# TensorE products whose results nobody reads, placed ahead of waits in the tail of a decode block

## The chip, the cores and the metric

The kernel runs on one core of one Trainium2 chip. The metric is the device time of one execution in microseconds, as the median of several runs. All data are 32-bit floats.

## What is computed

One token passes through an attention block with a cached context and then through a bilinear feed-forward block. The context has 65536 positions, 8 key/value heads and 32 query heads of 128 elements; the model width is 512 and the feed-forward width 1792.

```python
x = A_x
h = x + _A_ref(_layernorm(x, axis=-1), A_k_cache, A_v_cache, A_wq, A_wo)
h2 = h + _B_ref(_layernorm(h, axis=-1), B_w_gate, B_w_up, B_w_down)
...
    scores = jnp.einsum("bhqd,bhkd->bhqk", q, k) * (Dh ** -0.5)
    p = _softmax(scores, axis=-1)
    o = jnp.einsum("bhqk,bhkd->bhqd", p, v)
...
    g = jnp.einsum("bsd,df->bsf", x, w_gate)
    u = jnp.einsum("bsd,df->bsf", x, w_up)
    h = g * u
    return jnp.einsum("bsf,fd->bsd", h, w_down)
```

## The kernel before

**The stream.** Everything that the kernel reads from device memory goes through SyncE's queue in one fixed order into two large buffers, `kv[0]` and `kv[1]`, of 8 MB each: for each of the 8 heads four pieces of keys and four of values, in turn. A piece is issued when TensorE has finished with the buffer. The last piece of values comes in four parts (`V_CUTS`). Behind it come the feed-forward weights: the gate weights in one transfer, the up weights `wu` in three (`U_CUTS`, rows 0 to 2, 2 to 3, 3 to 4 of four), both into `kv[0]` (L153, L156), and the down weights `wd` in five (`D_CUTS`, chunks 0 to 6, 6 to 10, 10 to 12, 12, 13 of fourteen) into `kv[1]` (L160). Each part has its own semaphore (`s_wu`, `s_wd`).

**The heads.** A loop of eight passes runs on TensorE alone. In a pass the keys are multiplied (L346), VectorE and ScalarE make the softmax, its weights are transposed on TensorE into the banks `ptp` (L361), the values are multiplied (L374), and the head's output is turned and projected (L381, L387).

**The tail.** After the last head one chain remains. VectorE adds the rows up (L280); TensorE turns the row into a column and takes off the mean (L396, L398); the gate weights are multiplied (L409 with `psc[1]`); one product makes the variance (L415), ScalarE and VectorE the scale. The up weights are multiplied (L409 with `psc[0]`), four products for each of four rows `k`, with a wait for a weight piece ahead of rows 0, 2 and 3. VectorE multiplies the two rows in two halves (L303); that product is the gated row. TensorE turns it into columns (L421, L425, L428), VectorE copies these into `f_pad` (L307, L309), and the down weights are multiplied: fourteen chunks `c` of four products each, four column blocks of the array side by side (L439), with a wait ahead of each piece. VectorE copies the result (L311), and SyncE writes it out (L313).

A 32-bit product appears in the trace as two matmul records, each with a weight load. So the 56 down products are 112 records, eight for a chunk, and four up products are eight records. Transposes have one record.

Of the kernel before, what the change touches and what calls it, by code (L numbers as in the profile page):

```python
# [24 lines left out]
P = 128  # L25
# [14 lines left out]
V_CUTS = (0, 16, 24, 28, 32)  # L40
U_CUTS = (0, 2, 3, 4)
D_CUTS = (0, 6, 10, 12, 13, 14)


M_Q, M_K, M_MX, M_MB, M_T, M_L, M_V, M_PO, M_AT, M_HEAD = 1, 2, 6, 7, 8, 12, 13, 17, 18, 18
# [14 lines left out]
def body(nc, xc, xr, kT, v, wq0, wqo, wo7, wg, wu, wd, out):  # L60
    pe_e, dve_e, act_e, pool_e, sp = nc.tensor, nc.vector, nc.scalar, nc.gpsimd, nc.sync

    def tile(name, *shape):
        return nc.alloc_sbuf_tensor(name, list(shape), F32).ap()

    def bank(name):
        return nc.alloc_psum_tensor(name, [P, 512], F32).ap()
# [5 lines left out]
    ident, mean_m, ones, neg_mean = (tile(n, P, P) for n in ("ident", "mean_m", "ones", "neg_mean"))  # L73
# [8 lines left out]
    zeros = tile("zeros", P, 512)  # L82
# [15 lines left out]
    ptp = [bank(f"ptp{i}") for i in range(2)]  # L98
# [5 lines left out]
    def sem(name):  # L104
        sems.append(nc.alloc_semaphore(name))
        return sems[-1]
# [7 lines left out]
    s_wu = [sem(f"s_wu{i}") for i in range(len(U_CUTS) - 1)]  # L114
    s_wd = [sem(f"s_wd{i}") for i in range(len(D_CUTS) - 1)]
    s_x, s_xr, s_out = sem("s_x"), sem("s_xr"), sem("s_out")
# [3 lines left out]
    def pe_at(h, m):  # L120
        return M_HEAD * h + m
# [35 lines left out]
    sp.wait_ge(pe.sem, pe_at(LAST, M_V + 3))  # L157
    for p, (lo, hi) in enumerate(zip(D_CUTS, D_CUTS[1:])):
        cs = slice(lo * D, hi * D)
# [159 lines left out]

    mm = pe_e.matmul  # L320

    def take(s, n=1):
        pe_e.wait_ge(s, n).then_inc(s, -n)  # L323

# [4 lines left out]
    mm(sm[1][:, 0:1], mean_m, ln_s2, start=True, stop=True).then_inc(pre, 1)  # L329
    pe_e.wait_ge(dve.sem, c_const)  # L330
    take(s_wq, 16)

    def head():
        for r in range(REP):
            for k in range(KT):
                i = mm(sm[0][:, r:r + 1], wq_sb[:, k, r * P:(r + 1) * P], xn[:, k:k + 1],  # L336
                       start=(k == 0), stop=(k == KT - 1))
        i.then_inc(pe.sem, 1)
        take(tok)
        for s in range(NT):  # L340
            take(s_kv[s % 2], 16)
            if s >= 2:
                take(tok)
            for rs in range(8):
                for j in range(4):
                    i = mm(psc[s % 2][32 * j:32 * j + 32, :],  # L346
                           q_pad[:, 28 - 4 * rs:60 - 4 * rs],
                           kv[s % 2][:, (4 * rs + j) * 512:(4 * rs + j + 1) * 512],
                           start=(rs == 0), stop=(rs == 7))
            i.then_inc(pe.sem, 1)  # L350
# [50 lines left out]
    def project(acc, w, sems):  # L401
        for k in range(KT):
            if len(sems) == 1 and k == 0:
                pe_e.wait_ge(sems[0], 16)
            elif len(sems) > 1 and k in U_CUTS:
                pe_e.wait_ge(sems[U_CUTS.index(k)], 16)
            for j in range(4):
                o = k * F + j * FJ
                i = mm(acc[32 * j:32 * j + 32, :FJ], hn_pad[:, k, :], w[:, o:o + FJ],  # L409
                       start=(k == 0), stop=(k == KT - 1))  # L410
        i.then_inc(pe.sem, 1)

    project(psc[1], wg_t, [s_wg])
    pe_e.wait_ge(dve.sem, c_s3)
    mm(sm[0][:, 0:1], mean_m, ln_s3, start=True, stop=True).then_inc(pe.sem, 1)  # L415
    for j in range(4):
        mm(pva[32 * j:32 * j + 32, 0:P], sel_pad, arow[:, j * P:(j + 1) * P], start=True, stop=False)
    project(psc[0], wu_t, s_wu)
    pe_e.wait_ge(dve.sem, c_f[0])
    for b in range(2):  # L420
        i = mm(sm[0][:, 4 * b:4 * b + 4], f_sb[:, b * P:(b + 1) * P], sel_q,  # L421
               start=(b == 0), stop=(b == 1))
# [4 lines left out]
    for i in range(2):  # L427
        i2 = mm(sm[1][64 * i:64 * i + 64, 4:6], f_sb[:, 3 * P:FJ], sel_q[:, 2 * i:2 * i + 2],  # L428
                start=False, stop=True)
    i2.then_inc(pe.sem, 1)  # L430
    pe_e.wait_ge(dve.sem, c_fp0)
    for c in range(NC):
        if c == 8:
            pe_e.wait_ge(dve.sem, c_fp1)
        if c in D_CUTS:
            pe_e.wait_ge(s_wd[D_CUTS.index(c)], 16)
        for j in range(4):
            o = c * D + j * P
            i = mm(pva[32 * j:32 * j + 32, 0:P], f_pad[:, c, :], wd_t[:, o:o + P],  # L439
                   start=False, stop=(c == NC - 1))  # L440
# [43 lines left out]
```

## Time and profile before

| | us |
|---|---|
| median of 3 runs (lowest to highest) | 1312.81 (1312.80 to 1312.94) |
| the profiled execution's own time | 1313.45 |
| its span, from the first to the last instruction | 1312.1 |
| TensorE matmul busy in the span | 717.8 |
| mean granted TensorE clock, as a share of full speed | 0.732 |

The profile shows one execution on the core. Its own time is 1.35 us longer than the span, which starts with the first instruction and ends with the last. [...] An end of a matmul record is modelled, and lies some tenths of a microsecond after the next product could start.

### The profile page before, as it was taken

What the parts mean: (1) busy time and instruction counts of PE and PEld (TensorE: products, weight loads), DVE (VectorE), ACT (ScalarE), POOL (GpSimd) and SP (SyncE); (2) the same over time, 40 slices, a digit from 0 to 9 for tenths busy, and PEclk for the clock granted to TensorE, in tenths of its full rate; (3) what the DMA queues carried; (4) which work ended last, traced back from release to release, by engine and by line L of the source; (5) the groups of instructions that cost most, each with busy time, mean ns of one, the idle gap of its engine ahead of it and who ended that gap; (6) DMA issues with size and microseconds to landing.
All of it is one profiled execution on the core that took longest, in us unless ns stands there. A gap on an engine that the chain in (4) does not pass through costs nothing. (4 is left out here: it accounts for less than half of the span.)

```text
span 1312.1 us, 10526 instructions
## 1 busy us (share of the span) xinstructions
PE 717.8 (55%) x4922; PEld 249.1 (19%) x4922; DVE 73.3 (6%) x180; ACT 47.2 (4%) x102; POOL 2.5 (0%) x13
## 2 busy tenths in 40 slices
PE   4355374553755446563574736735465454645657
PEld 3011031210312112120131201312121111211213
DVE  0000000100001000010000100001000010000101
ACT  0010000100001000010000100001000010000100
POOL 0000000000000000000000000000000000000000
PEclk9777676786767867767767767668677677777677
DMA  9999999999999999999999999999999999999998
GB/s 416 436 424 446 422 440 424 440 424 440 440 428 442 426 438 426 438 428 438 440 428 440 428 438 426 438 428 438 438 432 436 430 422 441 438 428 438 438 414 356
DMA packets 12405, 564.80 MB, mean 430 GB/s; under 512 B 1510, under 2 KB 1514, under 8 KB 2155
## 3 DMA queue, kind: packets, MB, share of 16 engines
q1 hardware_dynamic: 12248, 564.67, 99.6%
q8 instruction: 6, 0.10, 0.0%
q10 hardware_dynamic: 146, 0.00, 0.0%
q14 instruction: 5, 0.03, 0.0%
HBM read 564.66 MB, written 0.00 MB: 430 GB/s over the span
## 5 line engine op out<-in xcount | busy, mean ns | idle before, releaser
L346 PE MATMUL psc<-kv,q_pad 128*32 128x512 f32 x2048 | 296.8, 744 | 257.0 <-PEq L323 257.0
L374 PE MATMUL pva<-kv,pt 128*16 128x512 f32 x2048 | 283.1, 714 | 272.9 <-PEq L323 272.7
L346 PEld LDWEIGHTS psc<-kv,q_pad 128*32 128x32 f32 x2048 | 81.6, 133 | 465.7 <-issue 465.7
L374 PEld LDWEIGHTS pva<-kv,pt 128*16 128x16 f32 x2048 | 67.5, 111 | 492.0 <-issue 492.0
L224 ACT COPY sc<-psc 128x512 f32<-128x512 f32 x32 | 18.8, 586 | 1146.2 <-PE psc L346 1146.2
L230 DVE TENSOR_REDUCE mx<-sc 128x1 f32<-128x512 f32 x32 | 21.9, 686 | 541.2 <-ACT sc L224 541.2
L336 PE MATMUL sm<-xn,wqo_sb 128*128 128x1 f32 x256 | 48.8, 325 | 2.2 <-issue 2.2
L336 PEld LDWEIGHTS sm<-xn,wqo_sb 128*128 128x128 f32 x256 | 48.1, 293 | 9.6 <-issue 9.6
L264 DVE COPY orow<-pva 128x512 f32<-128x512 f32 x8 | 5.5, 692 | 566.6 <-PE pva L374 566.6
L361 PE MATMUL ptp<-ident,sc 128*128 128x128 f32 x128 | 29.2, 395 | 10.2 <-PEq L323 9.7
L361 PEld LDWEIGHTS ptp<-ident,sc 128*128 128x128 f32 x128 | 21.3, 201 | 15.5 <-issue 14.8
L249 ACT ACTIVATE sc<-sc,nbias 128x512 f32<-128x512 f32 x32 | 22.7, 711 | 20.2 <-DVE nbias L244 20.2
L254 DVE COPY pt<-ptp 128x512 f32<-128x512 f32 x32 | 22.1, 692 | 21.5 <-PE ptp L361 21.5
L366 PE MATMUL pva<-zeros 128*32 128x512 f32 x64 | 13.8, 948 | 0.0
L387 PE MATMUL attn<-wqo_sb,o_pad 128*32 128x512 f32 x64 | 10.9, 756 | 3.3 <-PEq L323 3.3
L381 PE MATMUL sm<-sel_b,orow 128*128 128x4 f32 x64 | 8.2, 252 | 7.2 <-PEq L323 7.2
L381 PEld LDWEIGHTS sm<-sel_b,orow 128*128 128x128 f32 x64 | 7.7, 191 | 14.4 <-issue 14.4
L352 PE MATMUL sm<-ident,m 128*1 128x128 f32 x8 | 2.2, 269 | 13.7 <-PEq L323 13.7
L364 PE MATMUL sm<-l,ones 128*128 128x4 f32 x16 | 4.1, 324 | 9.6 <-PEq L323 9.6
L409 PE MATMUL psc<-kv,hn_pad 128*32 128x448 f32 x64 | 8.9, 702 | 0.6 <-DMA kv<-in_wu 0.3
L439 PE MATMUL pva<-kv,f_pad 128*32 128x128 f32 x112 | 6.1, 416 | 1.1 <-DMA kv<-in_wd 1.1
L354 PE MATMUL sm<-ones,mexp 1*128 1x1 f32 x16 | 3.3, 276 | 5.7 <-PEq L323 5.7
(83 smaller groups left out, 67.7 us busy)
## 6 DMA issues: line engine op xcount, KB each, us to landing
wqo_sb<-in_wqo SPq DMA_DIRECT2D x7, 2048.0 KB, 14.0
kv<-in_v SPq DMA_DIRECT2D x1, 4096.0 KB, 22.5
kv<-in_wg SPq DMA_DIRECT2D x1, 3584.0 KB, 18.0
kv<-in_v SPq DMA_DIRECT2D x1, 2048.0 KB, 27.0
kv<-in_v SPq DMA_DIRECT2D x2, 1024.0 KB, 30.0
kv<-in_wu SPq DMA_DIRECT2D x1, 1792.0 KB, 22.4
kv<-in_wu SPq DMA_DIRECT2D x2, 896.0 KB, 24.9
kv<-in_wd SPq DMA_DIRECT2D x1, 1536.0 KB, 20.1
```

The costliest lines, as they stand in the source:

```text
L224: copies.append(act.tick(act_e.copy(sc[s], psc[s % 2])))
L230: i = dve_e.tensor_reduce(out=mx[:, s:s + 1], in_=sc[s], axis=AX.X, op=ALU.max)
L249: act_e.activation(sc[s], sc[s], AF.Exp, bias=nbias[:, 0:1], scale=SCALE, accum_out=sums[:, s:s + 1]).then_inc(atok, 1)
L254: dve_e.tensor_copy(pt[s].rearrange("p g b h -> p b g h"), ptp[s % 2].rearrange("p (b g h) -> p b g h", b=4, h=REP)).then_inc(tok, 1)
L336: i = mm(sm[0][:, r:r + 1], wq_sb[:, k, r * P:(r + 1) * P], xn[:, k:k + 1], start=(k == 0), stop=(k == KT - 1))
L346: i = mm(psc[s % 2][32 * j:32 * j + 32, :], q_pad[:, 28 - 4 * rs:60 - 4 * rs], kv[s % 2][:, (4 * rs + j) * 512:(4 * rs + j + 1) * 512], st ...
L361: i = pe_e.transpose(ptp[s % 2][:, b * P:(b + 1) * P], sc[s][:, b * P:(b + 1) * P], ident)
L366: mm(pva[32 * j:32 * j + 32, :], zeros[:, 0:32], zeros, start=True, stop=False)
L374: i = mm(pva[32 * j:32 * j + 16, :], pt[n][:, 8 * j + rs, :, :].rearrange("p b h -> p (b h)"), vt[:, w * 512:(w + 1) * 512], start=False, ...
L381: i = mm(sm[0][:, 0:REP], orow[:, b * P:(b + 1) * P], sel_b[:, 4 * b:4 * b + 4], start=(b == 0), stop=(b == 3))
L387: i = mm(attn[32 * r:32 * r + 32, :], o_pad[:, r, :], wo_sb[:, r, :], start=True, stop=True)
L409: i = mm(acc[32 * j:32 * j + 32, :FJ], hn_pad[:, k, :], w[:, o:o + FJ], start=(k == 0), stop=(k == KT - 1))
```

## The change

A function `fill(n)` issues `n` products of the identity matrix (stationary, 128x128) with 128 columns of zeros, into the transpose bank `ptp[0]`, which nothing reads in the tail. Fills are put ahead of waits on TensorE: 2 before the wait for up row 2, 3 before that for up row 3, 3 before the wait for the gated row, 4 before that for its first columns in `f_pad`, and 1, 0, 1 and 4 before those for the second to the fifth piece of the down weights. No wait is added, and no other engine's program is changed.

```diff
+U_FILL = (0, 2, 3)
+F_FILL = 3
+D_FILL = (4, 1, 0, 1, 4)
...
+    def fill(n):
+
+
+        for _ in range(n):
+            mm(ptp[0][:, 0:P], ident, zeros[:, 0:P], start=True, stop=True)
...
             elif len(sems) > 1 and k in U_CUTS:
+                fill(U_FILL[U_CUTS.index(k)])
                 pe_e.wait_ge(sems[U_CUTS.index(k)], 16)
...
     project(psc[0], wu_t, s_wu)
+    fill(F_FILL)
     pe_e.wait_ge(dve.sem, c_f[0])
...
     i2.then_inc(pe.sem, 1)
+    fill(D_FILL[0])
     pe_e.wait_ge(dve.sem, c_fp0)
     for c in range(NC):
         if c == 8:
             pe_e.wait_ge(dve.sem, c_fp1)
         if c in D_CUTS:
+            if c:
+                fill(D_FILL[D_CUTS.index(c)])
             pe_e.wait_ge(s_wd[D_CUTS.index(c)], 16)
```

On TensorE, from the up product to the last down product, the program before reads as follows (`psc` is the bank of the up product, `sm` that of the turned gated row, `pva` the result, `kv` the weights; a row with "waits" holds its semaphores).

```order
L409 MATMUL psc<-kv,hn_pad 32x448 [waits s_wu1]
L409 MATMUL psc<-kv,hn_pad 32x448 x3
L409 MATMUL psc<-kv,hn_pad 32x448 [waits s_wu2]
L409 MATMUL psc<-kv,hn_pad 32x448 x3
L421 MATMUL sm<-sel_q,f_sb 128x4 [waits dve]
...
L428 MATMUL sm<-sel_q,f_sb 64x2 x2
L439 MATMUL pva<-kv,f_pad 32x128 [waits s_wd0,dve]
L439 MATMUL pva<-kv,f_pad 32x128 x23
L439 MATMUL pva<-kv,f_pad 32x128 [waits s_wd1]
```

The same engine and place in the changed program, where each line below the new function has a number that is 10 to 15 higher (L330 is the product in `fill`):

```order
L330 MATMUL ptp<-zeros,ident 128x128 x2
L420 MATMUL psc<-kv,hn_pad 32x448 [waits s_wu1]
L420 MATMUL psc<-kv,hn_pad 32x448 x3
L330 MATMUL ptp<-zeros,ident 128x128 x3
L420 MATMUL psc<-kv,hn_pad 32x448 [waits s_wu2]
L420 MATMUL psc<-kv,hn_pad 32x448 x3
L330 MATMUL ptp<-zeros,ident 128x128 x3
L433 MATMUL sm<-sel_q,f_sb 128x4 [waits dve]
...
L440 MATMUL sm<-sel_q,f_sb 64x2 x2
L330 MATMUL ptp<-zeros,ident 128x128 x4
L454 MATMUL pva<-kv,f_pad 32x128 [waits s_wd0,dve]
L454 MATMUL pva<-kv,f_pad 32x128 x23
```

The fills stand ahead of the waiting products, so they start without waiting for what these wait for, and the products behind them start after them.

The end of TensorE's program, with the last three pieces of the down weights, in the changed kernel:

```order
L454 MATMUL pva<-kv,f_pad 32x128 [waits s_wd2]
L454 MATMUL pva<-kv,f_pad 32x128 x7
L330 MATMUL ptp<-zeros,ident 128x128
L454 MATMUL pva<-kv,f_pad 32x128 [waits s_wd3]
L454 MATMUL pva<-kv,f_pad 32x128 x3
L330 MATMUL ptp<-zeros,ident 128x128 x4
L454 MATMUL pva<-kv,f_pad 32x128 [waits s_wd4]
L454 MATMUL pva<-kv,f_pad 32x128 x3
```

Before, the same rows stand there as L439 without the two rows of L330; nothing has changed places. In all 18 fills are added, 36 matmul records.

## Rows read from the trace of the kernel before

**Rows 1.** The page: span, granted clock and transfers in 40 slices, memory traffic.
```profile
span 1312.1 us, 10526 instructions
...
PEclk9777676786767867767767767668677677777677
DMA  9999999999999999999999999999999999999998
...
HBM read 564.66 MB, written 0.00 MB: 430 GB/s over the span
```

**Rows 2.** The chain that ended last: start us, us, what.
```profile
1283.72 20.06 DMA kv<-in_wd
...
1303.91 6.12 PE pva L439 x112
...
1310.06 0.29 DVE y L311
```

**Rows 3.** Timeline of the tail: start, us, engine, line, output and inputs, records.
```profile
1284.56 1.03 PE L381 MATMUL sm<-sel_b,orow 128*128 128x4 f32 x8 [0.89 <-PEq L323]
...
1297.38 2.44 PE L409 MATMUL psc<-kv,hn_pad 128*32 128x448 f32 x24
...
1300.14 0.96 PE L409 MATMUL psc<-kv,hn_pad 128*32 128x448 f32 x8 [0.32 <-DMA kv<-in_wu]
1301.25 0.81 DVE L303 SCALAR_TENSOR_TENSOR f_sb<-psc,ln_r,g_sb 128x256 f32<-128x256 f32 x2 [3.55 <-PE psc L409]
...
1301.79 0.61 PE L421 MATMUL sm<-sel_q,f_sb 128*128 128x4 f32 x4 [0.69 <-DVE f_sb L303]
...
1302.55 0.28 PE L428 MATMUL sm<-sel_q,f_sb 128*64 128x2 f32 x4
1302.88 0.17 DVE L309 COPY f_pad<-sm 128x6 f32<-128x6 f32 x1 [0.28 <-PE sm L428]
...
1303.91 6.08 PE L439 MATMUL pva<-kv,f_pad 128*32 128x128 f32 x112 [1.08 <-DMA kv<-in_wd]
```

**Rows 4.** The down weights' transfers: issue times, and us from issue to landing.
```profile
L160 SPq DMA_DIRECT2D kv<-in_wd x5: 328/432/433, 1283.7 to 1285.5; - x5
...
DMA to landing us min/median/max: 20.1/23.0/23.3
```

**Rows 5.** Timeline of SyncE's queue: starts of the second and the fourth issue.
```profile
1284.09 0.91 SPq L160 DMA_DIRECT2D kv<-in_wd  x2
...
1285.04 0.91 SPq L160 DMA_DIRECT2D kv<-in_wd  x2
```

**Rows 6.** Transfers by issue: second, third and fourth down piece, us to landing last.
```profile
kv<-in_wd SPq DMA_DIRECT2D x1, 1024.0 KB, 22.2
...
kv<-in_wd SPq DMA_DIRECT2D x1, 512.0 KB, 23.0
...
kv<-in_wd SPq DMA_DIRECT2D x1, 256.0 KB, 23.1
```

**Rows 7.** The up weights' transfers, as in group 4.
```profile
L156 SPq DMA_DIRECT2D kv<-in_wu x3: 432/432/432, 1273.4 to 1274.3; - x3
...
DMA to landing us min/median/max: 22.4/24.1/25.8
```

**Rows 8.** Stretches: length, busy of PE, PEld, DVE, ACT, POOL, then granted clock, DMA.
```profile
1282.50:1285.80 3.30, 2.08 (x16) 1.13 (x16) 0.80 (x2) 0.00 (x0) 0.00 (x0) 1.00 1.01 434
...
1291.40:1296.00 4.60, 4.60 (x28) 1.28 (x32) 0.28 (x2) 0.00 (x0) 0.00 (x0) 0.50 0.97 404
1296.40:1299.80 3.40, 3.40 (x42) 1.19 (x34) 0.16 (x1) 0.90 (x2) 0.00 (x0) 1.00 1.04 435
1299.80:1302.80 3.00, 1.99 (x22) 1.10 (x18) 0.98 (x3) 0.00 (x0) 0.00 (x0) 1.00 0.97 410
1303.00:1309.60 6.60, 5.68 (x108) 5.64 (x112) 0.05 (x1) 0.00 (x0) 0.00 (x0) 0.50 0.63 247
```

**Rows 9.** Transposes (L361) of the last head in a stretch: PE, PEld, granted clock, DMA.
```profile
1218.40:1220.40 2.00, 1.94 (x8) 1.41 (x8) 0.50 1.06 459
```

## The prediction

> **What bounds the kernel now.** I read the page first: the transfers are busy in nine tenths or more of every slice but the last, 430 GB/s over the span [rows 1]. The kernel is bound by one stream of 565 MB, and nothing in the diff touches it. So the change can only work behind the stream's end, and I looked there with the chain of waits. It says that after the first down piece has landed (1283.72 + 20.06 = 1303.78) one thing alone sets the end: 6.12 us of down products, then the copy and the write [rows 2]. About 2 us pass from the copy's start at 1310.06 to the span's end at 1312.1.
>
> Is that stage held by its own work or by the later pieces? The issues start at 1284.09 and 1285.04 for the second and fourth piece [rows 5], so the third starts half way, at 1284.56, and the fifth at 1285.5 [rows 4]. With their times to landing [rows 4, 6] the pieces land at 1306.29, 1307.56, 1308.14 and 1308.8. The products go without a gap from 1303.91 for 6.08 us, fourteen chunks at 0.434 us [rows 3]; they reach chunks 6, 10, 12 and 13 at 1306.51, 1308.25, 1309.12 and 1309.55, always after the piece. So TensorE's own pace sets the end, but the last piece is not far ahead: by 0.75 us.
>
> The stretches say why the pace is what it is. [...] At full clock a chunk should take half, 0.217 us; rows at both levels say so for the up product: the gate products before 1296 run at half the pace of the up products behind them (28 records in 4.6 us against 42 in 3.4, some of these small) [rows 8].
>
> **The price of a fill.** The trace has no such product. It is two passes of 128 columns with a 128-column weight load each. A down chunk is also two passes of 128 columns (four column blocks side by side): 0.434 us cold, 0.217 us warm. Does the wider load add to it? Eight transposes, with loads and columns of this size, took 1.94 us at half clock, 0.243 us each with the run-out of the last one in it [rows 9]. So the loads lie beside the products. At full clock, products with such loads and almost no columns took 1.03 us for eight records [rows 3], 0.129 a pass, 0.26 a fill. I take 0.22 warm and 0.44 cold, since the transposes are nearest in shape. The bounds: 0.26 by the load row; if load and columns did not overlap, 0.129 + 0.109 a pass, 0.47 a fill; and nothing, where waits cover every fill.
>
> **Up stage.** From two rows of up products (three rows `k` and a run-out are 2.44 us, one row and a run-out 0.96 [rows 3]) a row takes 0.74 us. Before, row 2 starts at 1297.38 + 1.48 = 1298.86 and its piece has been there since about 1298: the second issue, half way between 1273.4 and 1274.3, and 24.1 us [rows 7]. So the first two fills fall in no wait and cost 0.44 us in full. Row 2 then runs from 1299.30 to 1300.04, three fills to 1300.70. Piece 3 landed at 1274.3 + 25.8 = 1300.1 [rows 7]; row 3 starts at 1300.70 instead of 1300.14. **The gated row is 0.56 us later.** Row 3 ends at 1301.44, the next three fills at 1302.10; VectorE's first half is done for TensorE at 1301.79 + 0.56 = 1302.35, so these three are hidden with 0.25 us to spare.
>
> **Down stage.** The last turning products end at 1302.55 + 0.28 + 0.56 = 1303.39. Four fills take 0.88 us, to 1304.27. By then the first piece is there (1303.78), and so are both copies into `f_pad` (1302.88 + 0.17 + 0.56 = 1303.61). The first chunk starts 0.36 us later than before. If the clock has stayed up: six chunks (1.30) to 1305.57, a fill to 1305.79, wait for the piece: 1306.29 and the 0.13 us that lay between landing and product before, 1306.42. Four chunks to 1307.29, wait to 1307.56 + 0.13 = 1307.69, two chunks to 1308.12, a fill to 1308.34 (the piece is there at 1308.27), a chunk to 1308.56. Now four fills, 0.88 us, to 1309.44, though the last piece has been usable since 1308.93: half a microsecond given away. The last chunk ends at 1309.66. Before it was 1303.91 + 6.08 = 1309.99. **Gain 0.33 us.**
>
> With a fill at 0.26 the same count ends at 1309.86 (gain 0.13), with fills at nothing at 1308.93 + 0.22 = 1309.15 (gain 0.84). At 0.47 the three hidden fills become late too (row 3 ends at 1302.69, fills at 1304.10 against 1303.60), the down stage starts at 1307.02 and ends at 1312.88, a loss of 2.9 us; the transposes' row speaks against that price.
>
> The profiled execution took 1313.45 us, span 1312.1 and 1.35 around it; by the sum that is 1313.1. It was 0.64 above the median of the runs shown, so the median goes from 1312.81 to 1312.5.
>
> **Rivals.** 0.2% of this kernel, about what a measurement can tell from no change, is 2.6 us.
>
> (a) *Nothing to win back.* In the median run the clock may not have fallen where it did in the profiled one. The profiled time is 0.64 above the median; a down stage at full clock, waiting only for pieces, would end at 1309.15, 0.84 earlier, which is of this size. Then the fills only cost: 1309.66 against 1309.15, 0.5 us slower (0.7 with a fill at 0.26), 1313.3 to 1313.5. For it: the falls near 1285.8 and after 1302.8 followed stretches of nearly the same busy share, so a small shift of the moment could change the case. Against it: three runs within 0.14 us.
> [...]
>
> (b) *The fills don't hold the clock, and only delay* (the other side). If products of zeros don't keep it up, it falls at 1302.8 as before. From 1303.39 four cold fills (1.76) put the first chunk at 1305.15; every chunk takes 0.434, every fill 0.44, and no piece is waited for: 1305.15 + 14 x 0.434 + 6 x 0.44 = 1313.87. That is 3.9 us slower, 1316.7, or 0.3%. It decides if the clock falls before about 1304.5 and stays down. Against: the fills add eight products, 1.76 us at full clock, between 1298.9 and 1302.1, where TensorE had 1.99 of 3 us, much of it in loads and run-outs; stretches as full as that had the clock up [rows 8].
> [...]
>
> (c) *The last piece sets the end.* With the clock up the stage could be bound by landings; then 1309.15, 0.84 us faster, 1312.0. The four fills before the last piece speak against it, unless a fill takes under 0.1 us.
>
> **How the numbers follow.** Forecast, clock held and fills mostly paid (1311.9 to 1312.8 for it alone): 0.50. (a) 0.33. (c) 0.06. (b) 0.05. The rest, 0.06, is for a stream that runs differently in another program, as likely to be shorter as longer. No case but (b), its price bound and half of that rest reaches 0.2% either way: faster 0.03, same 0.92, slower 0.05. The range takes in (c) with the spread of the runs below it, 1311.7, and (a) with the same above it, 1313.8.
>
> **What would show it.** In the trace after: granted clock 1.0 from the up product to the end of the down products; row 3 of the up product some 0.56 us later beside its transfer; the turning products 0.56 us later; chunks at 0.22 us with two short waits for pieces; the last four fills ending after the last piece has landed; a copy of the result 0.1 to 0.8 us earlier. The prediction is wrong if the clock falls in the down stage in spite of the fills, if a fill takes 0.4 us or more at full clock, or if the time moves by more than 2.6 us, which the tail can't give.

## The result and the profile after

The changed kernel took **1314.47 us** (median of 22 runs, 1313.82 to 1316.11) against 1312.78 us (22 runs, 1312.53 to 1313.12): ratio 1.0014, 95% interval 1.0008 to 1.0020. It is 1.7 us slower. That is less than 0.2% of the kernel, but clear of the noise, on the other side of the forecast, and 0.7 us above the range. The profiled execution took 1314.29 us, span 1313.0 us.

The chain that ended last in the changed kernel, from the up product on (start, us, what; `ptp L330` are fills, `psc L420` the up product, `pva L454` the down product):

```profile
1297.69 1.50 PE psc L420 x16
1299.19 0.64 PE ptp L330 x4
1299.83 0.89 PE psc L420 x8
1300.72 0.86 PE ptp L330 x6
1301.59 0.89 PE psc L420 x8
1302.48 0.86 PE ptp L330 x6
1303.34 0.43 PE sm L433 x4
1303.78 0.22 PE sm L437 x2
1304.00 0.21 PE sm L440 x4
1304.21 1.09 PE ptp L330 x8
1305.30 1.45 PE pva L454 x48
1306.75 0.42 PE ptp L330 x2
1307.17 1.45 PE pva L454 x48
1308.61 0.42 PE ptp L330 x2
1309.03 0.36 PE pva L454 x8
1309.39 1.09 PE ptp L330 x8
1310.48 0.40 PE pva L454 x8
```

Where the chain of before began with a transfer [rows 2], this one has no transfer and no wait: TensorE works from the up product to the end, two fifths of the time on fills. The forecast had the gated row 0.56 us later than before; it is 1.39 us later (L433 starts at 1303.18 in the timeline, L421 stood at 1301.79 [rows 3]). The first down chunk is 1.3 us later instead of 0.36. Four starts in the timeline of the changed kernel, which the rest goes by (first up product, first turning product, first and last down chunk; in the chain above the same work starts some hundredths to tenths later):

```profile
1297.50 1.69 PE L420 MATMUL psc<-kv,hn_pad 128*32 128x448 f32 x16
...
1303.18 0.60 PE L433 MATMUL sm<-sel_q,f_sb 128*128 128x4 f32 x4
...
1305.23 1.52 PE L454 MATMUL pva<-kv,f_pad 128*32 128x128 f32 x48
...
1310.41 0.43 PE L454 MATMUL pva<-kv,f_pad 128*32 128x128 f32 x8
```

A count of records tells what a fill costs. One fill has two records; groups of 1, 2, 3 and 4 took 0.42, 0.64, 0.86 and 1.09 us. That is 0.22 us a fill, as forecast, **plus 0.2 us for the group**. The up rows ahead of a group took 0.89 us instead of 0.74: the fills start when the product before them has all but run out (at 1299.12 in the timeline, where the up product's modelled end is 1297.50 + 1.69 = 1299.19). The load unit shows the same place (timeline of weight loads; the bracket is its idle time before):

```profile
1299.12 0.52 PEld L330 LDWEIGHTS ptp<-zeros,ident 128*128 128x128 f32 x4 [0.73 <-issue]
1299.76 0.16 PEld L420 LDWEIGHTS psc<-kv,hn_pad 128*32 128x32 f32 x8
...
1306.68 0.30 PEld L330 LDWEIGHTS ptp<-zeros,ident 128*128 128x128 f32 x2 [0.20 <-issue]
```

The first load of a fill starts at the moment at which the fill itself is shown to start, and the load unit idles until then, 0.73 and 0.20 us. So in this trace the load was not fetched while the products before it ran, and the next up row's load in turn started behind the loads of the fills, at 1299.76 with its product.

The clock and the transfers of the changed kernel, in two views (stretches, with the granted clock third from the end; issues and landings of the down weights):

```profile
1301.60:1305.20 3.60, 3.60 (x32) 2.73 (x32) 1.15 (x4) 0.00 (x0) 0.00 (x0) 1.00 0.98 406
1305.30:1310.80 5.50, 5.50 (x124) 4.30 (x124) 0.00 (x0) 0.00 (x0) 0.00 (x0) 1.00 0.36 137
```

```profile
L164 SPq DMA_DIRECT2D kv<-in_wd x5: 328/432/433, 1284.0 to 1285.8; - x5
...
DMA to landing us min/median/max: 19.7/22.6/23.0
```

The clock is at 1.0 to the end, as forecast, where rows 8 had 0.5. The last piece lands at 1285.8 + 23.0 = 1308.8 us, the same as before. Its product starts 1.6 us later.

### The profile page after: what moved, and what is told of

Same layout as the page of the kernel before. It is cut to its first block, busy times and chain, and to the rows that moved or that the text cites. A ratio compares the mean times of both kernels' runs of the same rounds, so it can differ in the third digit from the quotient of the medians.

```text
span 1313.0 us, 10598 instructions
## 1 busy us (share of the span) xinstructions
PE 719.7 (55%) x4958; PEld 251.3 (19%) x4958; DVE 73.3 (6%) x180; ACT 47.2 (4%) x102; POOL 2.5 (0%) x13
## 5 line engine op out<-in xcount | busy, mean ns | idle before, releaser
L391 PE MATMUL sm<-sel_b,orow 128*128 128x4 f32 x64 | 8.5, 256 | 7.2 <-PEq L333 7.2
L391 PEld LDWEIGHTS sm<-sel_b,orow 128*128 128x128 f32 x64 | 8.0, 196 | 14.4 <-issue 14.4
L420 PE MATMUL psc<-kv,hn_pad 128*32 128x448 f32 x64 | 8.7, 671 | 0.3 <-DVE hn_pad L290 0.3
L374 PEld LDWEIGHTS sm<-l,ones 128*128 128x128 f32 x16 | 3.6, 280 | 12.6 <-issue 12.6
```

The costliest lines, as they stand in the source:

```text
L391: i = mm(sm[0][:, 0:REP], orow[:, b * P:(b + 1) * P], sel_b[:, 4 * b:4 * b + 4], start=(b == 0), stop=(b == 3))
```

## The experiments

Two theories stood at first. **A fixed price of a group**: each group of fills costs some 0.35 us on top of its fills. **Nothing to win back**, rival (a): the typical execution of before has its clock up already. For the fixed price two causes were then tested against each other: **form**, a change between products on one column block and fills on the whole array, and the run-out of any extra group, whatever its form. The kernel before, run beside them, had a median of 1312.75 us (33 runs) with the first four, 1312.73 (21) with the two of column-block fills, and 1312.79 (33) with the last four.

**The kernel before once more** (`base_again`, no edit).

> The kernel before, unchanged, to see the span and the granted clock of each of its runs. If the typical run of before already keeps the clock up in the down stage (theory 'nothing to win back'), its spans lie near 1311.4 us, 0.7 under the 1312.1 of the profiled one, and the down products take about 5.2 us with waits for pieces instead of 6.08 us at half clock. If the profiled execution was typical, the spans lie near 1312.1 us. Ratio to before 1.000 either way.

1312.73 us, ratio 1.0001 (0.9992 to 1.0010), span 1311.4. Its down stage in the timeline, and the stretch:

```profile
1298.54 3.19 PE L409 MATMUL psc<-kv,hn_pad 128*32 128x448 f32 x32
...
1303.93 1.52 PE L439 MATMUL pva<-kv,f_pad 128*32 128x128 f32 x48 [0.46 <-DMA kv<-in_wd]
1306.33 1.08 PE L439 MATMUL pva<-kv,f_pad 128*32 128x128 f32 x32 [0.88 <-DMA kv<-in_wd]
1307.58 1.07 PE L439 MATMUL pva<-kv,f_pad 128*32 128x128 f32 x24 [0.17 <-DMA kv<-in_wd]
1308.86 0.43 PE L439 MATMUL pva<-kv,f_pad 128*32 128x128 f32 x8 [0.21 <-DMA kv<-in_wd]
```

```profile
1303.90:1309.20 5.30, 4.01 (x112) 2.78 (x112) 0.00 (x0) 0.00 (x0) 0.00 (x0) 1.00 0.63 246
```

Here the clock is up without a fill, and TensorE waits for four of the five pieces (the fourth, chunk 12, is there in time, inside the row of 24 records). The last piece sets the end; two lines of the chain that ended last show its transfer and the chunk behind it:

```profile
1286.39 22.43 DMA kv<-in_wd
...
1308.86 0.47 PE pva L439 x8
```

The piece lands at 1308.82, and the chunk starts 0.04 us later. This is a typical execution: its time, 1312.74 us, lies at the median. The execution from which the prediction was made took 1313.45 us; of the 87 runs of the kernel before beside the experiments 12 lie above 1313.2 us, and of the 11 here 3. Of the twelve traces taken in all, that first one alone has the clock at 0.5 in the down stage, after a fall near 1302.9. Whether it fell in the other long runs too isn't on record.

**Only the up fills** (`up_only`).

```diff
-F_FILL = 3
-D_FILL = (4, 1, 0, 1, 4)
+F_FILL = 0
+D_FILL = (0, 0, 0, 0, 0)
```

> Only the five fills in the up stage. Theory 'each group of fills costs a fixed 0.35 us beside 0.21 us a fill': the gated row comes 1.2 to 1.3 us later, the first down chunk at about 1304.3 instead of 1303.9 us since the first piece hides the rest, and the median is 0.3 to 0.8 us over before. Rival 'a fill costs 0.22 us and no more': the gated row is 0.56 us later, hidden behind the first down piece, no change.

1312.71 us, ratio 0.9999 (0.9990 to 1.0008). The delay is there and the loss is not; in the timeline of this kernel:

```profile
1304.41 1.52 PE L454 MATMUL pva<-kv,f_pad 128*32 128x128 f32 x48
...
1306.30 1.08 PE L454 MATMUL pva<-kv,f_pad 128*32 128x128 f32 x32 [0.38 <-DMA kv<-in_wd]
```

The first chunk starts half a microsecond later than before (1304.41 against 1303.91), as expected, without a wait, and the second piece is waited for all the same. The expected loss of 0.3 to 0.8 us took it that a late first chunk reaches the end; it doesn't as long as a later piece is waited for.

**Only the fills around the gated row** (`row_only`).

```diff
-U_FILL = (0, 2, 3)
+U_FILL = (0, 0, 0)
-D_FILL = (4, 1, 0, 1, 4)
+D_FILL = (4, 0, 0, 0, 0)
```

> Only the three fills ahead of the gated row and the four behind its turning. Both groups lie in waits of before (0.9 and 1.1 us). Fixed cost theory: the first chunk starts 0.2 to 0.3 us later, the clock stays up, the pieces set the end: 0.2 to 0.8 us under the profiled execution of before, between -0.2 and +0.3 us against its median. Rival 'fills hold the clock only as an unbroken chain from the up stage on': clock falls near 1303, down products at half clock from about 1304.2, 0.3 to 1 us slower than before.

1312.78 us, ratio 0.9999 (0.9990 to 1.0008): no cost, no gain. The granted clock is 1.0 from 1303.9 to 1309.2, so the rival, which had it fall near 1303, is out.

**Only the fills between the down pieces** (`down_only`).

```diff
-U_FILL = (0, 2, 3)
-F_FILL = 3
-D_FILL = (4, 1, 0, 1, 4)
+U_FILL = (0, 0, 0)
+F_FILL = 0
+D_FILL = (0, 1, 0, 1, 4)
```

> Only the six fills between the down pieces. With the clock up at the start of the stage, fixed cost theory gives an end near 1310.5 us in the timeline, 0.5 us over the profiled execution of before; with the clock down at the start the fills cost double, and the end is 1.5 to 4 us over it. So 0.5 to 4 us slower, with a wide spread between runs. Rival 'a fill costs 0.22 us and no more': 0 to 2.5 us slower.

1313.99 us (1313.80 to 1314.64), ratio 1.0010 (1.0001 to 1.0019): 1.24 us, three quarters of the loss, though only six of the 18 fills are there. The spread is 0.8 us, not wide.

**Only the last four fills** (`last4_only`).

```diff
-U_FILL = (0, 2, 3)
-F_FILL = 3
-D_FILL = (4, 1, 0, 1, 4)
+U_FILL = (0, 0, 0)
+F_FILL = 0
+D_FILL = (0, 0, 0, 0, 4)
```

> Only the four fills ahead of the last down piece. In the typical run of before the last chunk waits 0.21 us for its piece, which lands near 1308.8 us. The four fills take 1.09 us and begin when the chunk before has run out, near 1308.6, so they end 0.8 to 1 us after the landing. Theory 'the delay of the change is fills behind the last waits, put directly on the end': 0.7 to 1.1 us slower than before (1313.4 to 1313.9), most of the 1.24 us that the six down fills cost. Rival 'the delay comes from the sum of all groups': under 0.4 us.

1313.69 us, ratio 1.0009 (1.0000 to 1.0018), 0.90 us. The end of its chain:

```profile
1307.74 1.05 PE pva L454 x24
1308.80 1.09 PE ptp L330 x8
1309.88 0.40 PE pva L454 x8
```

The fills start at 1308.73 in the timeline, shortly before the last piece lands (1286.4 + 22.6 = 1309.0). So some 0.2 to 0.3 us of their 1.09 lie where TensorE waited before, and the rest goes to the end, as the median says. This one group is over half of what the change costs.

**The change without its last four fills** (`no_last4`).

```diff
-D_FILL = (4, 1, 0, 1, 4)
+D_FILL = (4, 1, 0, 1, 0)
```

> The change without its last four fills. In the profiled execution of the change the last chunk would start at 1309.39 instead of 1310.41 us, 1.0 us earlier, and still 0.5 us behind the landing. So 0.9 to 1.2 us faster than the change (1313.2 to 1313.6), 0.5 to 0.9 us slower than before, and still with a wide spread since nothing in the tail waits. Rival 'the last fills are all of the cost': equal to before within 0.15 us.

1313.16 us (1312.67 to 1313.88), ratio 1.0004 (0.9995 to 1.0013). 1.13 us below the change, run beside it on the same chip (`after_again`, below), as expected; 0.37 above before, a little less than expected. The interval against before holds 1, so only the step from the change is clear: of the 11 runs of each, only two of this kernel (1313.87 and 1313.88) lie above the lowest of the change (1313.85).

**Fills in the form of their neighbours** (`tiled_fill`).

```diff
-            mm(ptp[0][:, 0:P], ident, zeros[:, 0:P], start=True, stop=True)
+            for j in range(4):
+                mm(ptp[0][32 * j:32 * j + 32, 0:P], ident[:, 0:32], zeros[:, 0:P], start=True, stop=True)
```

> The change with every fill made of four products on the four column blocks of the array (32 columns of identity each), the form of the up and down products, instead of one on the whole array; the same counts and places. Theory 'a change between whole-array and column-block products waits for the run-out and then for a weight load, 0.35 us a group': the groups then cost 0.21 us a fill, the tail is as the prediction had it, 1.2 to 2 us faster than the change (1312.5 to 1313.3 us). Rival 'any extra group costs its run-out, whatever its form': as the change, 1314.3 to 1314.6 us.

1313.38 us (1313.01 to 1314.08), ratio 1.0004 (0.9995 to 1.0013): 1.1 us below the change, a little less than the 1.2 to 2 expected, and 0.65 above before. The chain shows the groups at their bare price (eight records a fill now):

```profile
1300.43 0.44 PE ptp L331 x16
1300.87 0.75 PE psc L421 x8
1301.62 0.66 PE ptp L331 x24
1302.27 0.75 PE psc L421 x8
...
1308.61 0.22 PE ptp L331 x8
1308.83 0.22 PE pva L455 x8
1309.05 0.87 PE ptp L331 x32
1309.92 0.26 PE pva L455 x8
```

Groups of 1, 2, 3 and 4 take 0.22, 0.44, 0.66 and 0.87 us, and an up row 0.75 us again. The other group of four, behind the turning products of 64 columns, took 1.01 us in this chain; there the form still changes. Same bank, same counts, same places: only the form differs, so the theory of form stands, and "any group costs its run-out" falls.

**Such fills only in waits of before** (`tiled_gaps`), with the edit of `tiled_fill` and

```diff
-U_FILL = (0, 2, 3)
+U_FILL = (0, 0, 1)
-D_FILL = (4, 1, 0, 1, 4)
+D_FILL = (4, 0, 0, 0, 0)
```

> Column-block fills only where TensorE waited before: one ahead of up row 3, three ahead of the gated row, four behind its turning, none between the down pieces. If the fixed cost is one of form, none of these delays the chain by over 0.2 us, the clock stays up to the end, and the pieces set the end at about 1309.2 us of the timeline: 0.6 to 0.8 us under the profiled execution of before, 0 to 0.4 us under its median (1312.4 to 1312.8 us), spread as narrow as that of before. Rival 'before has nothing to win back': equal to before within 0.1 us. Rival 'any group costs its run-out': 0.2 to 0.6 us over the median of before.

1312.79 us (1312.61 to 1312.93), ratio 1.0000 (0.9991 to 1.0009). Equal to before within 0.06 us: there is nothing to win back in the typical run. None of its 11 runs, nor of those of `up_only` and `row_only`, lies above 1312.94, where 12 of 87 of before lie above 1313.2. That suggests that fills ahead of the down pieces do spare the rare long execution. But none of the 22 runs of before beside the change lies above 1313.12 either, and no second long execution of before was traced, so it isn't shown.

**Four more fills at the head** (`late_after`), and **the change once more** (`after_again`, no edit).

```diff
-U_FILL = (0, 2, 3)
+U_FILL = (4, 2, 3)
```

> The change with four more fills ahead of the first up row, a delay of 1.1 to 1.2 us at the head of the chain. Theory 'the fills have eaten every wait, so any delay ahead of the tail reaches the end': 1.1 to 1.2 us slower than the change (1315.5 to 1315.8). Rival 'waits for pieces still absorb': 0.0 to 0.4 us. In the kernel before such a delay is absorbed: the five up fills alone cost 1.27 us there and moved nothing.

> The changed kernel, unchanged, for a second trace and the span and clock of its runs. Theory 'the moment at which the clock rises ahead of the up product moves from run to run, and in the changed kernel that shift reaches the end': times again spread over 1313.8 to 1316 us, and in the trace the end lies as much later or earlier than 1310.9 us as the first up product lies later or earlier than 1297.5. Rival 'the spread comes from the transfers': the end moves, the first up product does not.

`late_after` 1315.40 us (1314.38 to 1317.21), ratio 1.0022 (1.0013 to 1.0031); `after_again` 1314.29 us (1313.85 to 1315.89), ratio 1.0013 (1.0004 to 1.0022). The four fills cost 1.11 us, as the theory of eaten waits said; the five of `up_only` cost more delay (the gated row starts 5.66 us after the up product there, 3.88 in `base_again`) and lost nothing, because waits lay behind them. Two lines of the chain of `late_after`, then four of the timeline of `after_again`:

```profile
1299.67 1.64 PE psc L420 x16
...
1312.60 0.40 PE pva L454 x8
```

```profile
1296.36 1.69 PE L420 MATMUL psc<-kv,hn_pad 128*32 128x448 f32 x16
...
1306.29 1.08 PE L454 MATMUL pva<-kv,f_pad 128*32 128x128 f32 x32 [0.27 <-DMA kv<-in_wd]
1307.54 0.65 PE L454 MATMUL pva<-kv,f_pad 128*32 128x128 f32 x16 [0.17 <-DMA kv<-in_wd]
...
1309.97 0.43 PE L454 MATMUL pva<-kv,f_pad 128*32 128x128 f32 x8
```

In the chain of `late_after` 12.93 us lie between the starts of the first up product and of the last chunk, in the changed kernel 1310.48 - 1297.69 = 12.79, nearly a fixed length. In `after_again` the up product starts 1.14 us earlier than in the first trace of the change, but the last chunk only 0.44 us earlier: two waits for pieces are back. So the expectation for `after_again` held for the spread, and for the trace in direction only: the transfers do set a floor in the early executions.

## Why the prediction was wrong

**What bounds the kernel: wrong for the typical run.** The step "TensorE's own pace sets the end" was true of the one execution in the trace [rows 2, 8] and not of the median: `base_again` shows waits for four of the five pieces and an end set by the last landing. The prediction saw that the profiled time was 0.64 us above the median and carried it along as an offset. It was the clock, 0.50 against 1.00 from 1303.9 to 1309.2: the two traces of the kernel before differ by 0.7 us at the end of the down products (1309.99 against 1309.29) and by 0.71 in their times. By the sum's own count the last chunk of the typical execution starts at 1308.93; it started at 1308.86. Rival (a), at 0.33, was the case. Its price of 0.5 to 0.7 us is near what `tiled_fill` measured, 0.65, but partly by luck: the count has two waits for pieces, and in the trace of `tiled_fill` the up product starts 1.4 us later than counted, at 1298.74, and no piece is waited for.

**The price of a fill: right per fill, short per group.** 0.22 us stands. The step that failed is the one from the transposes to the fills, "so the loads lie beside the products": the transposes of rows 9 follow one another on the whole array, so they could not show what a change of form costs, and the sum put it at nothing. It is 0.35 us a group: 0.2 in the group itself and 0.14 for the row ahead of it (0.89 against 0.75).

**The up stage.** Forecast 0.56 us, measured 1.39 to the gated row, of which 0.12 came with the head of the tail (up product at 1297.50 instead of 1297.38). The two groups explain 2 x 0.35 = 0.70 of the 0.71 us between 1.27 and 0.56. Alone this costs nothing (`up_only`).

**The down stage.** "Half a microsecond given away" at the last four fills was the right place, with too small a size: 0.90 us alone (`last4_only`), where the fills start at 1308.73 instead of 1308.56 and take 1.09 us instead of 0.88. In the change the last chunk starts at 1310.41 instead of 1309.44. It then takes 0.43 us to its end and not 0.22, since no chunk behind it covers its run-out: the sum left that out, so its gain of 0.33 us was 0.2 too high by itself.

**The sum.** The forecast gain of 0.33 us was measured from an end of 1309.99. In the typical execution 0.7 of it was not there to win (1309.29 in `base_again`). The end of the change came 1.2 later than counted (1310.84 against 1309.66): 0.2 is the run-out of the last chunk, 0.1 the later head, and the rest, about 0.9, the form, as far as no wait took it up. That makes a loss of 1.55 us between the ends of the two traces and of 1.7 between the medians. The medians of the runs split it in another way: 1.1 us go when the fills have the form of their neighbours (`tiled_fill`), and 0.65 is left for the fills themselves.

**Rival (b)** fell: the clock stayed up, at 1.0, from the up product to the last chunk in both traces of the change. That the fills held it is not shown by this, since it stays at 1.0 without them in `base_again`. **Rival (c)** fell for the change, and describes the kernel before.

**The spread.** Nothing in the prediction had it. Before absorbs a late up product (1298.54 in `base_again` against 1297.38 in the first trace) by its waits; the changed kernel does not. The traces have the first up product between 1296.31 (`no_last4`) and 1298.74 (`tiled_fill`) in kernels that agree up to there, 2.4 us apart, and the change's times lie 2.3 us apart. That shift goes with the clock, and most of it arises before the up stage. Behind the last values of the heads the granted clock falls near 1283.0 us in `base_again`, `tiled_fill` and `last4_only`, near 1285.5 in the first trace of the change, and near 1287.2 in `after_again` and `no_last4`. The same eight turning products of the last head (L381 and L391) take 1.84 us behind an early fall and 1.03 ahead of a late one, in `base_again` and `after_again`:

```profile
1285.44 1.84 PE L381 MATMUL sm<-sel_b,orow 128*128 128x4 f32 x8 [0.88 <-PEq L323]
...
1284.66 1.03 PE L391 MATMUL sm<-sel_b,orow 128*128 128x4 f32 x8 [0.89 <-PEq L333]
```

The gate product then starts at 1293.07 in `base_again` and at 1291.24 in `after_again`, 1.8 us apart, and the up product 2.2 us apart. The rest goes with the rise: in `after_again` the clock is 1.0 in the stretch from 1294.5 to 1296.2, in `base_again` 0.5. No run set the moment of the fall on purpose, so that the clock causes the shift is argued from these rows and not tested.
Why the moment of the fall moves, by 4 us between these traces, they don't show.

## What to carry to other kernels

Before filling a wait, look at several executions: if the profiled one lies above the usual times, its stall may be the exception. A fill is only free where a wait behind it, at once or later in the chain, is longer than the delay in the worst execution: here the up fills alone moved nothing, and four fills at the head of a tail without waits cost 1.11 us. Ahead of the last piece of this transfer-bound kernel that wait was 0.2 us, and what the fills took beyond it went to the end. If TensorE must be kept busy between column-block products, use products of the same form: here groups of n of them took 0.22 n us, and groups on the whole array cost 0.35 us more.

## What the hardware showed unexpectedly

A change between products on one 32-column block and products on the whole array cost about 0.35 us there and back at a granted clock of 1.0: groups of n fills took 0.2 + 0.22 n us and the products ahead 0.14 us more, against 0.22 n and nothing in the same form. The load unit shows the change of form too. In the change the first load of a fill starts with its product (both at 1306.68 for the second group of the down stage). In `tiled_fill` the load of the same group starts 0.11 us ahead of its product:

```profile
1306.79 0.24 PEld L331 LDWEIGHTS ptp<-zeros,ident 128*32 128x32 f32 x8
...
1306.90 0.40 PE L331 MATMUL ptp<-zeros,ident 128*32 128x128 f32 x8
```

That the later load is the cause was not tested apart, and neither was a rival: the fills of `tiled_fill` also have narrower loads (32 columns instead of 128), so no run tells the width of a load from the change of form.
